# Fewer sums behind the last loads, a new deal of the last stores, and a rearranged order of steps in a fused attention and feed-forward kernel

## The chip, the cores and the metric

The kernel runs on one core of a Trainium2 chip. The metric is the device time of one execution in microseconds (us); the time of a kernel is the median of its runs. Engines are named as in the profile: PE is TensorE's matrix multiplication (PEld its weight loads), DVE is VectorE, ACT is ScalarE, POOL is GpSimd, and SP is SyncE, which here only issues transfers. ACT and POOL issue transfers too.

## The reference

Two layers, one behind the other, on q, k, v of [4, 6080, 256] in fp32, with tau = 1:

```
qn, kn = q / |q| , k / |k|                  # norms over the 6080 tokens, per channel
a      = softmax(kn^T qn / tau, last axis)  # 256 x 256 for each of the 4 batches
x      = v @ a                              # [24320, 256] over all batches
out    = gelu_tanh(x @ w_in) @ w_out        # w_in 256 x 2048, w_out 2048 x 256, out in fp32
```

The kernel computes in bf16 with fp32 sums and uses that x @ w_in = v @ (a @ w_in): for each batch it makes the 256x2048 matrix "aw" = a @ w_in once and multiplies v by it.

## The kernel before

**Blocks.** The 24,320 tokens are cut into 25 blocks: five of 1024 and one of 960 for each batch, the last batch ending in 512 and 448. A block goes through two products. The first, v @ aw followed by gelu, gives g; the second, g @ w_out, gives the output. Both are built mostly by a Strassen-like scheme (fewer products of quarters, more sums): m1 to m7 and the steps with a leading w (wcq, wap, wax, wy5, and wGp, wGs, wGr, wGx, the gelus) belong to the first product, T1 to T4 (sums over tokens), M1 to M7 and cq, y5, ap, ax, c11 to c22 to the second. Some parts of the first product are made plainly: "g.u_x" is a plain product (`plain`), "G.u_x" its gelu. M7 reads the sum T3. In blocks 1 to 22 T3 is made by a transfer on POOL's queue that adds in place (g<-g, `token_sum`, `SUMS_DMA`), everywhere else by DVE. The last block, 24, has a plain second product, `direct` (words "D.p_t").

**Output.** A step c11, c12, c21 or c22 turns a quarter of a block's output by a DVE transpose into an output tile (`turn`, L748; tag "ot", three buffers). When both quarters of a half are in, `store` (L754) issues four transfers of that half, one for each 32 partitions. Before, blocks 0 to 23 store on SP's queue; block 24 has the words sB (half 0) and sA (half 1), each with two stores on SP's queue and two on ACT's, in turn.

**Order.** From the end of the front on, what each engine does and when is not found at run time. A string `ORDER` of some 3,950 words is written out by hand; `run` executes one word after another, and each engine gets its own instructions in that order. A word is "what.arguments@bank:block". Loads of q, k and v for later batches (lq, lk, lv, lt) stand in it as well and wait for the PE instruction that was issued last.

**The front.** The first batch is done by code of its own ahead of ORDER (L791 to L869). q and k come in six chunks of 8, 7, 8, 8, 8, 8 rows (a row is 128 tokens); the last chunk comes in five pieces in the order q 0-3, k 0-4, k 5-7, q 4-5, q 6-7. For each chunk, `gram_row` adds a row's k and q to the gram matrix G on PE; `early_squares` squares q on ACT and k on DVE; `early_fold` (chunks 0 to 3) adds the two halves of the squares on DVE; `ss_rows` sums squares over tokens on PE, 256 columns for a row of k and two single columns for a row of q. Chunk 4's squares are not folded, so it has 8 row sums each for k and q. `warm` issues filler products of 256 columns on PE. Behind the last chunk:

```
scores(0):    lnk, rk from the k sums; lnq, rq from the q sums; S = G * rk; eT = exp(S * rq)
first_aw():   row sums of eT and the first 512 columns of a @ w_in on PE;
              rs = 1 / row sums on DVE; four pieces of aw out of PSUM, (f, ic):
              (0, 0) DVE, (0, 1) ACT, (1, 0) DVE, (1, 1) DVE; each 128 x 256
```

Block 0's first 512 tokens of v are transposed on PE (`pe_vt`), and two copies (`pe_vt_copy`, vT<-vt_ps) bring them to SBUF, both on DVE. ORDER then begins with plain products of block 0 (h<-vT,aw, four groups of 128 columns for each 512 of aw) and with the words aw.p and ac.p, which make and copy the other slices of aw. Its first words are

```
g.3_0@f:0 g.0_0@g:0 g.2_0@a:0 aw.2@b:0 aw.3@c:0 ac.2:0 ac.3:0 g.1_0@d:0 vp.1@z:0 vc.1_1:0 vc.1_0:0
```

Of the kernel before, what the change touches and what calls it, by code (L numbers as in the profile page):

```python
# [16 lines left out]
def kernel(  # L17
# [446 lines left out]
    def pe_vt_copy(n, h, cc):  # L464
        x, y = parts_of(n)[h]
        nc.vector.tensor_copy(vt_tile(n)[:, cc, x:y], VPS[n, h][:, cc, :])
# [277 lines left out]
    def turn(n, ci, tj, src):  # L744
# [6 lines left out]
        if TURNED[n, tj] == 2 and n != LAST:  # L751
            store(n, tj, (nc.sync,) * 4)

    def store(n, tj, engines):  # L754
# [4 lines left out]
        dst = out[r0 : r0 + hc, :].rearrange("(x t) (b c) -> b t x c", t=32, b=4)
        for bi in range(4):  # L760
            engines[bi].dma_start(
                out=dst[bi],
                in_=ot[bi * 32 : bi * 32 + 32, 0 : hc // 32].rearrange("p x h c -> p x (h c)"))
# [197 lines left out]
vp.0@z:1 g.12_1@e:0 g.11_1@a:0 g.10_0@c:0 pA11:0 pS3:0 vc.0_0:1 G.5_1:0 g.6_1@f:0 G.11_1:0 G.4_1:0
G.14_1:0 G.10_0:0 g.8_0@b:0 G.12_1:0 lq.0:1 g.0_1@a:0 g.9_1@d:0 g.15_1@g:0 g.6_0@c:0 g.8_1@e:0
G.0_1:0 G.9_1:0 pF0:0 g.7_1@a:0 lv.1:1 G.6_0:0 G.6_1:0 G.8_1:0 vc.0_1:1 g.13_1@d:0 G.7_1:0 G.13_1:0
pS1:0 SW.1:0 pF1:0 T1.1:0 T1.0:0 pS4:0 M1.1@c:0 g.3_0@f:1 G.15_1:0 g.4_0@e:1 pNA:0 G.4_0:1 lq.1:1
g.15_0@a:0 G.3_0:1 g.12_0@d:1 g.0_0@g:1 M1.0:0 g.11_0@e:0 G.8_0:0 lt.1:1 T2.0:0 g.10_0@f:1 T3.1:0
pA12:0 G.11_0:0 G.12_0:1 G.10_0:1 ksq.0:1 M5.1@b:0 M5.0:0 lv.0:2 y5:0 G.15_0:0 qsq.0:1 row.0_2@z:1
T2.1:0 g.13_0@e:0 f1.0:1 row.0_1:1 row.0_4:1 g.2_0@d:1 g.14_0@f:0 m1.1@b:1 G.0_0:1 G.2_0:1 pS2:0
f2.0:1 vs:1 lq.2:1 g.12_0@a:0 f3.0:1 T3.0:0 g.8_0@g:1 G.14_0:0 G.12_0:0 wcq.1@d:1 row.0_3:1 G.8_0:1
row.0_0:1 g.4_1@f:1 row.0_5:1 m2.1:1 g.7_1@a:1 lk.2:1 G.13_0:0 g.10_1@g:1 G.4_1:1 m1.5@e:1 row.1_3:1
row.1_1:1 row.1_5:1 wGp.1:1 cq@f:0 g.3_1@d:1 row.1_4:1 row.1_0:1 row.1_2:1 G.10_1:1 G.7_1:1 m5.1@g:1  # L970
lq.3:1 G.3_1:1 gc:1 wy5.1:1 wcq.5@a:1 m6.1:1 M6.0:0 m5.5@d:1 M6.1:0 wap.1@g:1 T4.1:0 m2.5:1 wy5.5:1
sp.0@z:1 lv.1:2 wGp.5:1 sa.0:1 ksq.1:1 qsq.1:1 ap@d:0 m6.5:1 M2.0:0 g.15_1@a:1 M2.1:0 lk.3:1 f1.1:1
c11:0 f2.1:1 G.15_1:1 m3.1:1 m7.1:1 g.0_1@a:1 wax.1:1 wGs.1:1 M3.1:0 G.0_1:1 f3.1:1 T4.0:0 g.2_1@g:1
lt.1:2 m1.6@c:1 m5.6@a:1 M7.1:0 sp.1@z:1 m4.1:1 G.2_1:1 lt.0:2 M7.0:0 M3.0:0 wy5.6:1 sa.1:1
g.15_0@g:1 wap.5@a:1 ksq.2:1 m7.5:1 wGr.1:1 qsq.2:1 m3.5:1 lk.4:1 ax:0 f1.2:1 wGx.1:1 wax.5:1
G.15_0:1 M4.1:0 wcq.6@b:1 f2.2:1 g.7_0@g:1 wGs.5:1 c12:0 f3.2:1 m2.6:1 wGx.5:1 m6.6:1 m4.5:1
g.11_1@a:1 G.7_0:1 lq.4:1 wap.6@d:1 M4.0:0 sp.2@z:1 g.11_0@g:1 wGr.5:1 G.11_1:1 wGp.6:1 m7.6:1
g.12_1@e:1 T1.0:1 c21:0 sa.2:1 M5.0@a:1 qsq.3:1 m3.6:1 row.2_0@z:1 wax.6:1 ksq.3:1 G.12_1:1 wGs.6:1
m4.6:1 T1.1:1 g.8_1@b:1 f1.3:1 row.2_3:1 vs:2 wGx.6:1 wGr.6:1 g.0_0@f:2 row.3_2:1 G.11_0:1 G.8_1:1
lv.0:3 g.4_1@e:2 T2.1:1 lk.5:1 m1.3@d:2 G.4_1:2 row.3_1:1 g.4_0@c:2 wcq.3@g:2 M5.1:1 m5.1@b:2  # L980
m5.3@e:2 m2.3:2 G.0_0:2 row.2_5:1 y5:1 T2.0:1 wy5.3:2 G.4_0:2 wy5.1:2 row.2_2:1 m1.1@f:2 m6.3:2
T3.1:1 g.12_0@a:2 row.3_5:1 g.8_1@e:2 row.2_1:1 row.3_0:1 wap.3@c:2 wcq.1@b:2 m6.1:2 row.3_4:1
G.8_1:2 lq.5:1 wap.1@e:2 G.12_0:2 m2.1:2 wGp.3:2 f2.3:1 m7.3:2 row.3_3:1 m3.3:2 wax.3:2 row.2_4:1
M1.0@a:1 m5.2@g:2 m3.1:2 m7.1:2 M1.1:1 gc:1 wGs.3:2 f3.3:1 T4.0:1 lv.1:3 m1.5@c:2 sp.3@z:1 m4.3:2
wGx.3:2 wGp.1:2 wy5.2:2 wGs.1:2 g.12_1@b:2 T3.0:1 wax.1:2 cq@g:1 ksq.4:1 qsq.4:1 m4.1:2 M2.1:1
wGr.3:2 wcq.5@e:2 G.12_1:2 wGr.1:2 m1.2@d:2 m2.5:2 wcq.2@b:2 M2.0:1 m5.5@f:2 lq.6:1 sa.3:1 f1.4:1
m6.2:2 m2.2:2 wGp.5:2 m1.6@e:2 M6.0:1 m6.5:2 wy5.5:2 wcq.6@f:2 lk.6:1 c11:1 wGp.2:2 f2.4:1 wap.2@a:2
T4.1:1 m3.2:2 m7.2:2 m2.6:2 wGx.1:2 wax.2:2 g.0_1@b:2 M6.1:1 wGs.2:2 m4.2:2 wGp.6:2 G.0_1:2
wap.5@a:2 f3.4:1 m6.6:2 ap@f:1 c22:0 wGr.2:2 wGx.2:2 m5.6@b:2 m3.5:2 lt.0:3 sp.4@z:1 ksq.5:1 m7.5:2
m1.7@d:2 M7.1:1 wax.5:2 qsq.5:1 f1.5:1 sa.4:1 f2.5:1 lt.1:3 M3.1:1 M7.0:1 m4.5:2 wGs.5:2 wcq.7@a:2  # L990
wy5.6:2 M3.0:1 m6.7:2 ax:1 m5.7@b:2 f3.5:1 wGr.5:2 wy5.7:2 m2.7:2 sp.5@z:1 M4.0:1 wGx.5:2 wap.6@c:2
sa.5:1 m7.6:2 wap.7@b:2 wax.6:2 qsq.6:1 wGp.7:2 row.4_2@z:1 row.4_3:1 m3.7:2 m7.7:2 c12:1 ksq.6:1
M4.1:1 lk.7:1 wGx.6:2 wGs.7:2 wax.7:2 m3.6:2 row.5_0:1 g.8_0@f:2 m4.6:2 wGs.6:2 row.5_3:1 wGr.6:2
wGx.7:2 row.4_1:1 row.4_0:1 row.5_1:1 row.5_4:1 m4.7:2 row.5_5:1 row.4_4:1 row.4_5:1 m1.1@a:3
m1.2@b:3 G.8_0:2 wGr.7:2 c21:1 wcq.1@c:3 f1.6:1 g.0_0@g:3 g.8_1@e:3 vs:3 f2.6:1 m2.1:3 m5.1@f:3
wcq.2@d:3 lq.7:1 G.8_1:3 T1.0:2 wy5.1:3 row.5_2:1 m2.2:3 m6.1:3 M1.1@e:2 wap.1@f:3 wGp.2:3 wGp.1:3
G.0_0:3 m5.2@d:3 m6.2:3 m3.1:3 m7.1:3 T3.0:2 T1.1:2 g.0_1@c:3 wax.1:3 m1.3@g:3 wy5.2:3 wGs.1:3
G.0_1:3 M5.1@d:2 wap.2@f:3 m5.3@c:3 m3.2:3 m4.1:3 lv.0:4 wGx.1:3 M1.0:2 m7.2:3 f3.6:1 T2.0:2 gc:1
lv.1:4 wy5.3:3 wGr.1:3 wGs.2:3 wcq.3@c:3 wax.2:3 M5.0:2 m2.3:3 sp.6@z:1 cq@a:2 T2.1:2 m5.4@f:3
m4.2:3 y5:2 wGp.3:3 wy5.4:3 m6.3:3 wGr.2:3 wap.3@d:3 qsq.7:1 M2.0:2 M2.1:2 m7.3:3 m1.4@c:3 sa.6:1  # L1000
ksq.7:1 T3.1:2 lv.0:5 c11:2 M6.0:2 m1.5@f:3 m3.3:3 wcq.4@b:3 T4.0:2 m2.4:3 wGx.2:3 wax.3:3 wcq.5@e:3
# [333 lines left out]
```

## Time and the profile before

| what | us |
|---|---|
| median of 3 runs (lowest to highest) | 683.48 (683.37 to 683.81) |
| the profiled execution | 684.09 |
| its span, from the first to the last instruction | 682.3 |
| first plain product (h) starts | 38.23 |
| last product of PE ends | 675.7 |
| last stores: issued on ACT / SP from | 675.36 / 677.62 |

The profile is one execution, of 684.09 us, with 1.79 us around its span. A row of the timeline gives start, busy time, engine, line, operation, the tile written and the tiles read, sizes, count, and in brackets the idle time ahead of the group and what ended it. The windows give busy time and, in brackets, instructions of each engine in a stretch, then the granted PE clock (1.00 is full), the DMA share and GB/s. The tail of the span is in us: PE is done at 675.7, and what is left is turning and storing block 24.

### The profile page before, as it was taken

Reading aid. Unit: us, or ns where it says so; the run is one execution under the profiler, and the core shown is the slowest. Engines: PE = TensorE matmul, PEld = TensorE weight load, DVE = VectorE, ACT = ScalarE, POOL = GpSimd, SP = SyncE. Lnnn points to the kernel's source line nnn. Section 1 sums busy time; section 2 is a strip of 40 time slices with the busy share of each in tenths; the row PEclk is TensorE's granted clock in tenths of the full one; section 3 lists DMA queues with packets and bytes.
Section 4 is the critical chain, followed back from the end, with each engine's and each line's share of the span. In section 5 each row is a group of like instructions: output and inputs, shape, how many; then the busy total and the mean of one; then the engine's idle time right before and its main releaser. Section 6 shows DMA issues by size and latency. Waiting matters only on the chain.

```text
span 682.3 us, 10610 instructions
## 1 busy us (share of the span) xinstructions
PE 663.0 (97%) x3579; PEld 336.3 (49%) x3579; DVE 612.2 (90%) x941; ACT 621.5 (91%) x1193; POOL 112.4 (16%) x177
## 2 busy tenths in 40 slices
...
GB/s 240 208 256 126 151 180 167 178 165 136 175 151 175 171 164 155 175 80 166 129 135 169 175 167 197 134 134 150 69 148 115 101 151 147 101 107 152 81 84 96
DMA packets 168807, 101.70 MB, mean 149 GB/s; under 512 B 150240, under 2 KB 153952, under 8 KB 168032
## 3 DMA queue, kind: packets, MB, share of 16 engines
...
q14 instruction: 27, 0.22, 0.1%
...
## 4 chain that ended last, share of the span: by engine, by line
PE 93%; DMA 3%; DVE 2%; ACT 0%; issue 0%; SPq 0%; POOL 0%; DVEq 0%; POOLq 0%
PE rb L481 18%; PE p L481 17%; PE q L481 15%; PE r L481 11%; PE h L481 10%; PE m L481 10%; PE G L205 6%; PE awp L375 2%; DMA qk_f<-in_q_dram 1%; DMA g<-g 1%; PE o L481 1%; PE warm L269 1%; PE ss L263 1%; DVE t L700 0%; DMA vT<-vb 0%; DVE q L622 0%
## 5 line engine op out<-in xcount | busy, mean ns | idle before, releaser
L481 PEld LDWEIGHTS <-wcomb 128*128 128x128 bf16 x1408 | 136.6, 98 | 144.9 <-issue 3.4
L631 ACT ACTIVATE g<-q 128x512 bf16<-128x512 f32 (+1 forms) x286 | 169.4, 623 | 5.7 <-PE q L481 5.1
L481 PEld LDWEIGHTS <-aw 128*128 128x128 bf16 x807 | 77.9, 98 | 77.1 <-DVE aw L415 1.3
L622 DVE TENSOR_TENSOR q<-rb,yw 128x512 f32<-128x512 f32 (+2 forms) x150 | 102.4, 687 | 13.3 <-PE rb L481 4.4
L700 DVE TENSOR_TENSOR t<-g,t 128x2048 bf16<-128x2048 bf16 (+2 forms) x96 | 112.7, 1180 | 0.1
L625 DVE TENSOR_TENSOR xw<-rb,yw 128x512 f32<-128x512 f32 (+2 forms) x150 | 101.5, 678 | 10.1 <-PE rb L481 7.5
L481 PE MATMUL rb<-tv,sw 128*128 128x512 bf16 (+3 forms) x314 | 109.2, 367 | 0.0
L539 ACT ACTIVATE g<-h 128x512 bf16<-128x512 f32 (+1 forms) x164 | 97.1, 650 | 5.3 <-PE h L481 5.1
L619 ACT ACTIVATE yw<-m 128x512 f32<-128x512 f32 (+2 forms) x150 | 93.0, 626 | 3.9 <-PE m L481 2.9
L481 PE MATMUL p<-t,wcomb 128*128 128x512 bf16 (+2 forms) x384 | 95.5, 373 | 0.0
L631 ACT ACTIVATE g<-xw 128x512 bf16<-128x512 f32 (+1 forms) x143 | 92.6, 650 | 2.7 <-DVE xw L625 2.3
L613 ACT ACTIVATE q<-rb 128x512 f32<-128x512 f32 (+2 forms) x150 | 90.6, 614 | 4.7 <-PE rb L481 3.0
L481 PE MATMUL r<-g,wcomb 128*128 128x512 bf16 (+2 forms) x384 | 94.7, 373 | 0.0
L481 PE MATMUL h<-vT,aw 128*128 128x512 bf16 (+2 forms) x336 | 93.5, 377 | 0.8 <-DVE aw L415 0.8
L481 PEld LDWEIGHTS <-sw 128*128 128x128 bf16 x628 | 61.2, 98 | 61.8 <-issue 1.2
L631 ACT ACTIVATE g<-rb 128x512 bf16<-128x512 f32 (+1 forms) x143 | 87.7, 619 | 2.5 <-PE rb L481 2.1
L694 POOL DMA_DIRECT2D g<-g x44 | 39.7, 917 | 196.3 <-ACT g L631 92.0
L700 DVE TENSOR_TENSOR t<-g 128x2048 bf16<-128x2048 bf16 (+2 forms) x48 | 56.4, 1184 | 1.6 <-ACT g L539 1.3
L481 PE MATMUL q<-vT,sw 128*128 128x512 bf16 (+3 forms) x157 | 56.2, 367 | 0.0
L481 PE MATMUL q<-vT,aw 128*128 128x512 bf16 (+3 forms) x157 | 55.8, 367 | 0.0
L481 PE MATMUL rb<-vT,aw 128*128 128x512 bf16 (+3 forms) x157 | 55.7, 367 | 0.0
L481 PE MATMUL m<-tv,sw 128*128 128x512 bf16 (+3 forms) x157 | 55.7, 367 | 0.0
...
## 6 DMA issues: line engine op xcount, KB each, us to landing
...
wst<-in_moe_w_out_dram POOLq DMA_DIRECT2D x2, 1024.0 KB, 10.4
```

What stands on the lines that cost most here:

```text
L205: nc.tensor.matmul(G[b][:, jc, :], lhsT=qt[:np_, r, jc * 128 : jc * 128 + 128], rhs=kt[:np_, r, :], start=first and jc == 0, stop=jc == 1, ...
L263: nc.tensor.matmul(SS[1], lhsT=ones_bf, rhs=sq[:, 256:512], start=c == 0 and r == 0, stop=end)
L375: nc.tensor.matmul(ps, lhsT=ET[b][:, jc, ic * 128 : ic * 128 + 128], rhs=win_bf[:, jc, fs * 512 : fs * 512 + 512], start=jc == 0, stop=jc ...
L481: GATE[0] = nc.tensor.matmul(*a, skip_group_check=True, **kw)
L539: nc.scalar.activation(g_half(n, u // 8)[:, x, u % 8], hp[:, :hc], AF.Gelu_apprx_tanh)
L613: nc.scalar.activation(Q[n, i, 0][:, :w], RB[n, i][:, :w], AF.Copy)
L619: nc.scalar.activation(YW[n, i][:, :w], M5.pop((n, i))[:, :w], AF.Copy)
L622: nc.vector.tensor_add(Q[n, i, 1][:, :w], RB[n, i][:, :w], YW[n, i][:, :w])
L625: nc.vector.tensor_add(XW[n, i][:, :w], RB[n, i][:, :w], YW.pop((n, i))[:, :w])
L631: nc.scalar.activation(g[:, t, k0], x[:, :w], AF.Gelu_apprx_tanh)
L694: nc.gpsimd.dma_start(out=o, in_=quarter(n, 1, 1, h), accum_op=ALU.add)
L700: (nc.vector.tensor_add if add else nc.vector.tensor_sub)(o, a, b)
```

## The change

1. `early_fold_k`: the two halves of chunk 4's squares of k are added on DVE, and chunk 4 has 4 row sums of k where it had 8.
2. Chunk 5: the k sums 0-4 and 5-7 stand behind gram rows 0-3, the q sums 0-5 come in one go behind rows 4 and 5.
3. `warm(8)` becomes `warm(6)`.
4. The second of the two copies of block 0's transposed v goes from DVE to ACT.
5. `token_sum` can make T2 by an accumulating transfer as well, for the blocks in `SUMS2_DMA`, which is empty.
6. `direct` gives each quarter of block 24's half 1 a bank of its own (words "D.p_1_m").
7. Stores: of block 23's half 1, stores 0 and 2 stay with SP at the turn, and 1 and 3 go to ACT at the word c11:24. In block 24, sB is all on SP's queue, and sA has three stores on ACT's and one on SP's.
8. ORDER is rearranged: its first 500 words, several stretches in the middle, and its end. It holds the same products; between the stretches it is the same word for word. Block 0 now begins with the plain products of column groups 0 and 1 of aw (g.0_0, g.1_0).

```diff
+    def early_fold_k(c):
+        k = [x[:, :, 256:512] for x in SQ[c]]
+        nc.vector.tensor_add(k[0], k[0], k[1])
...
+    def pe_vt_copy(n, h, cc, eng="dve"):
...
+        if eng == "act":
+            nc.scalar.activation(o, i, AF.Copy)
+        else:
+            nc.vector.tensor_copy(o, i)
...
-            store(n, tj, (nc.sync,) * 4)
+            store(n, tj, (nc.sync, None) * 2 if (n, tj) == (LAST - 1, 1) else (nc.sync,) * 4)
...
-            store(n, 1 if what == "sA" else 0, (nc.sync, nc.scalar, nc.sync, nc.scalar))
+            store(n, 1 if what == "sA" else 0, (nc.sync,) * 4 if what == "sB" else (nc.scalar,) * 3 + (nc.sync,))
...
+            if n == LAST and what == "c11":
+                store(LAST - 1, 1, (None, nc.scalar) * 2)
             if n == LAST:
-                src = ACC[n, tj][:, ci * hc : ci * hc + hc]
+                src = ACC[n, tj, ci] if tj else ACC[n, tj][:, ci * hc : ci * hc + hc]
...
             if c < nch - 2:
                 early_fold(c)
+            else:
+                early_fold_k(c)
...
-        ss_rows(c - 1, 1)
+        ss_rows(c - 1, 1, range(0, 4))
         ss_rows(c - 1, 0)
         early_squares(c, 0, 0, 4, "act")
         early_squares(c, 1, 0, 5, "dve")
         for i in range(4):
             gram_row(0, c, i)
-        ss_rows(c, 0, range(0, 4))
+        early_squares(c, 1, 5, 8, "dve")
         ss_rows(c, 1, range(0, 5))
-        early_squares(c, 1, 5, 8, "dve")
+        ss_rows(c, 1, range(5, 8))
         early_squares(c, 0, 4, 6, "dve")
-        ss_rows(c, 1, range(5, 8))
         for i in (4, 5):
             gram_row(0, c, i)
-        ss_rows(c, 0, range(4, 6))
+        ss_rows(c, 0, range(0, 6))
...
-        warm(8)
+        warm(6)
         pe_vt(0, 0, "e")
         scores(0)
         pe_vt_copy(0, 0, 0)
-        pe_vt_copy(0, 0, 1)
+        pe_vt_copy(0, 0, 1, "act")
         first_aw()
...
+SUMS2_DMA = {}
...
 ORDER = """
-g.3_0@f:0 g.0_0@g:0 g.2_0@a:0 aw.2@b:0 aw.3@c:0 ac.2:0 ac.3:0 g.1_0@d:0 vp.1@z:0 vc.1_1:0 vc.1_0:0
+g.0_0@f:0 g.1_0@g:0 g.3_0@a:0 aw.2@b:0 G.1_0:0 g.2_0@e:0 aw.3@c:0 ac.2:0 ac.3:0 vp.1@z:0 g.4_0@d:0
...
-D.7_1:24 c11:24 c21:24 c12:24 sB:24 c22:24 sA:24
...
+D.5_1_1:24 D.2_0:24 c21:24 D.3_1_0:24 D.4_1_0:24 c11:24 D.1_1_1:24 D.5_1_0:24 D.3_1_1:24 D.6_1_0:24
+D.2_1_0:24 D.6_1_1:24 D.2_1_1:24 c12:24 sB:24 c22:24 sA:24
```

More of the change, by code (lines that the diff above doesn't have):

```diff
@@ L687, in token_sum @@
         hc = hc_of(n)
+        by_dma = n in (SUMS_DMA if i == 3 else SUMS2_DMA if i == 2 else ())
         if i == 3:
             o = quarter(n, 0, 1, h)
-        else:
-            o = tp.tile([128, 4, 512], BF16, tag="tx" if i in (1, 4) else "ty", name=f"t{i}{h}_{n}")[:, :, :hc]
+        elif i == 2 and by_dma:
+            o = TS[n, 1, h]
+        else:
+            x = i == 1 or i == 4 and n not in SUMS2_DMA
+            o = tp.tile([128, 4, 512], BF16, tag="tx" if x else "ty", name=f"t{i}{h}_{n}")[:, :, :hc]
         TS[n, i, h] = o
-        if i == 3 and n in SUMS_DMA:
+        if by_dma:
             nc.gpsimd.dma_start(out=o, in_=quarter(n, 1, 1, h), accum_op=ALU.add)
@@ L726, in next_sum, with direct @@
         fill(ACC[n, acc], tag, hc)
-    def direct(n, p, t, tag):
+    def direct(n, p, t, *mt):
         hc = hc_of(n)
-        for m in range(2):
-            first = (n, t) not in ACC
+        *ms, tag = mt
+        key = (n, t, *ms)
+        for m in ms or range(2):
+            first = key not in ACC
             if first:
-                ACC[n, t] = bank(tag, [128, 512], f"o{n}_{t}")
+                ACC[key] = bank(tag, [128, 512], f"o{n}_{t}_{m}")
                 BITS[tag] = 2 * hc
+            x0 = 0 if ms else m * hc
             for fc in (2 * p, 2 * p + 1):
                 w = ((A11, A12), (A21, A22))[m][fc // 8]
-                mm(ACC[n, t][:, m * hc : m * hc + hc], lhsT=wcomb[:, w, fc % 8, :],
+                mm(ACC[key][:, x0 : x0 + hc], lhsT=wcomb[:, w, fc % 8, :],
                    rhs=GT[n, fc // 8][:, t, fc % 8],
@@ L757, in store @@
         r0 = b * N + t0 + tj * hc
-        ot = OT.pop((n, tj))
+        ot = OT[n, tj]
         dst = out[r0 : r0 + hc, :].rearrange("(x t) (b c) -> b t x c", t=32, b=4)
         for bi in range(4):
-            engines[bi].dma_start(
-                out=dst[bi],
-                in_=ot[bi * 32 : bi * 32 + 32, 0 : hc // 32].rearrange("p x h c -> p x (h c)"))
+            if engines[bi] is not None:
+                engines[bi].dma_start(
+                    out=dst[bi],
+                    in_=ot[bi * 32 : bi * 32 + 32, 0 : hc // 32].rearrange("p x h c -> p x (h c)"))
     def mm2_step(n, what, tag):
@@ L961 @@
[L961 to L1001, printed above, removed]
@@ new lines @@
+M3.1:0 m4.5:1 qsq.2:1 g.12_1@e:1 wGp.6:1 ax:0 lq.4:1 m6.6:1 sa.1:1 ksq.2:1 wap.6@f:1 M4.0:0
+g.8_1@b:1 wGx.5:1 m7.6:1 wGr.5:1 f1.2:1 lq.5:1 wax.6:1 M3.0:0 g.11_1@g:1 G.8_1:1 f2.2:1 m3.6:1
+m4.6:1 G.12_1:1 wGx.6:1 G.11_1:1 c12:0 g.7_0@b:1 f3.2:1 M4.1:0 sp.2@z:1 lk.4:1 wGr.6:1 g.8_1@e:2
+g.4_0@d:2 vs:2 sa.2:1 m1.3@g:2 wGs.6:1 G.7_0:1 m5.3@c:2 g.12_0@f:2 row.2_2@z:1 T1.0:1 G.8_1:2 T3.0:1
+T1.1:1 wcq.3@b:2 wy5.3:2 G.4_0:2 row.2_5:1 m1.1@e:2 row.3_1:1 row.3_4:1 m6.3:2 row.3_0:1 c21:0
+m5.1@c:2 row.2_4:1 G.12_0:2 wcq.1@d:2 wap.3@f:2 lk.5:1 row.2_1:1 m2.1:2 qsq.3:1 m2.3:2 m7.3:2
@@ new lines @@
+ksq.4:1 m2.5:2 M2.0:1 wGs.2:2 wax.2:2 m4.2:2 f1.4:1 sa.3:1 m1.6@d:2 lk.6:1 M2.1:1 wGp.5:2 wGx.2:2
+wGr.2:2 ap@e:1 f2.4:1 wap.5@a:2 M7.0:1 f3.4:1 sp.4@z:1 wcq.6@b:2 qsq.5:1 M3.0:1 m7.5:2 c11:1 c22:0
+m2.6:2 ksq.5:1 lt.0:3 m3.5:2 m5.6@c:2 m6.6:2 wy5.6:2 wGs.5:2 M7.1:1 wax.5:2 m1.7@c:2 m4.5:2 f1.5:1
+wap.6@a:2 wGp.6:2 f2.5:1 wGr.5:2 wcq.7@b:2 wGx.5:2 M3.1:1 sa.4:1 f3.5:1 m7.6:2 m5.7@g:2 lt.1:3
+m3.6:2 m6.7:2 ax:1 wax.6:2 wy5.7:2 sp.5@z:1 m2.7:2 sa.5:1 M4.1:1 m4.6:2 c12:1 wap.7@g:2 M4.0:1
+T1.0:2 lk.7:1 c21:1 wGp.7:2 wGr.6:2 wGx.6:2 m3.7:2 g.8_0@b:2 row.5_0@z:1 m7.7:2 wGs.6:2 wax.7:2
@@ new lines @@
+wap.1@a:6 wcq.2@e:6 lq.3:2 wGr.3:6 m2.2:6 wGp.2:6 m5.2@c:6 m6.2:6 m7.1:6 wy5.2:6 m3.1:6 M6.1:5
+wGx.3:6 wGs.1:6 g.12_0@e:6 m5.5@c:6 M6.0:5 lk.3:2 G.12_0:6 g.12_1@a:6 c11:5 c22:4 f1.1:2 wax.1:6
+m4.1:6 wap.2@b:6 wy5.5:6 wGx.1:6 G.12_1:6 wGr.1:6 m1.5@e:6 m7.2:6 ap@c:5 M3.1:5 m3.2:6 wcq.5@a:6
+wax.2:6 wGs.2:6 m4.2:6 m6.5:6 m2.5:6 wGr.2:6 wGp.5:6 m5.6@g:6 T4.1:5 M3.0:5 wGx.2:6 wap.5@b:6 f2.1:2
+c12:5 m7.5:6 wax.5:6 m1.7@f:6 m3.5:6 row.1_3:2 m1.6@a:6 M7.1:5 wy5.6:6 m4.5:6 wcq.6@c:6 lk.4:2
+wGs.5:6 row.0_0:2 m6.6:6 wGr.5:6 m5.7@g:6 wcq.7@b:6 T4.0:5 M7.0:5 m2.6:6 wGx.5:6 f3.1:2 wap.6@e:6
@@ new lines @@
+wap.6@e:11 M6.0:10 m4.5:11 row.0_3@z:3 m6.7:11 m2.7:11 wy5.7:11 lv.1:14 ap@d:10 m3.6:11 m7.6:11
+row.0_4:3 wGr.5:11 M7.1:10 wGx.5:11 wGp.7:11 wap.7@g:11 wax.6:11 T4.1:10 m3.7:11 m4.6:11 m7.7:11
+M3.0:10 wGx.6:11 wax.7:11 c22:9 wGr.6:11 g.4_1@f:12 wGs.7:11 wGs.6:11 SW.0:2 M7.0:10 G.4_1:12 ax:10
+g.0_1@b:12 m1.3@g:12 G.0_1:12 m4.7:11 g.8_0@e:12 m1.1@f:12 wGr.7:11 wcq.1@b:12 wcq.3@a:12 M3.1:10
+vs:12 lt.1:13 G.8_0:12 M4.0:10 m2.1:12 m5.3@e:12 c12:10 m6.3:12 wGx.7:11 wy5.3:12 wGp.1:12 T1.1:11
+wap.3@d:12 lt.0:13 m2.3:12 M4.1:10 m5.1@e:12 g.0_0@b:12 m3.3:12 wGp.3:12 T1.0:11 G.0_0:12 m7.3:12
@@ new lines @@
+wcq.3@a:13 m1.5@c:13 sp.2@z:3 y5:12 c11:12 wcq.5@d:13 sa.2:3 m2.3:13 m6.3:13 m4.2:13 ksq.3:3 M6.0:12
+m6.5:13 m2.5:13 row.2_1@z:3 m1.6@f:13 wGp.3:13 wGr.2:13 wap.3@a:13 m3.3:13 row.2_0:3 m7.3:13
+wap.5@e:13 m3.5:13 wGx.2:13 M6.1:12 wGp.5:13 T4.1:12 lq.4:3 wcq.6@d:13 wGs.3:13 m6.6:13 m7.5:13
+row.3_4:3 wax.3:13 row.3_2:3 wGs.5:13 ap@a:12 T4.0:12 m4.3:13 m5.6@e:13 qsq.3:3 m2.6:13 M3.0:12
+wy5.6:13 lk.5:3 wGx.3:13 M3.1:12 wGp.6:13 wGr.3:13 wap.6@e:13 wax.5:13 c12:12 m7.6:13 row.3_0:3
+m5.7@d:13 m4.5:13 m1.7@b:13 g.4_1@a:13 M7.1:12 wGx.5:13 wGr.5:13 wcq.7@c:13 c22:11 wy5.7:13 wax.6:13
@@ new lines @@
+wap.3@e:14 ap@d:13 f3.4:3 m7.3:14 c11:13 lt.0:15 lt.1:15 m3.3:14 m1.6@b:14 wGs.3:14 wcq.6@g:14
+M3.1:13 sp.4@z:3 wax.3:14 qsq.5:3 M7.1:13 m6.6:14 m5.7@e:14 ksq.5:3 wy5.7:14 M7.0:13 m4.3:14
+wap.6@c:14 lv.1:16 f1.5:3 m2.6:14 m7.6:14 m1.7@e:14 ax:13 m3.6:14 wGr.3:14 wcq.7@a:14 wGx.3:14
+wGs.6:14 f2.5:3 sa.4:3 M3.0:13 M4.1:13 f3.5:3 c12:13 wax.6:14 sp.5@z:3 g.12_0@c:14 m2.7:14 m6.7:14
+wGp.6:14 M4.0:13 lq.7:3 qsq.6:3 sa.5:3 ksq.6:3 row.4_5@z:3 g.4_0@d:14 row.5_0:3 wap.7@g:14 m7.7:14
+m4.6:14 row.5_2:3 m3.7:14 row.5_1:3 wGx.6:14 f1.6:3 row.4_0:3 wGp.7:14 G.12_0:14 row.5_5:3
@@ new lines @@
+sa.7:3 T4.1:14 wy5.6:15 lv.0:17 m1.6@c:15 m7.4:15 pow:3 m5.7@b:15 m3.4:15 wax.4:15 wcq.6@g:15
+lv.0:18 wGs.4:15 M7.0:14 m4.4:15 m6.6:15 c12:14 ax:14 wap.6@a:15 m1.7@d:15 wy5.7:15 wGr.4:15
+g.0_0@b:15 m2.6:15 wcq.7@e:15 G.0_0:15 row.6_5@z:3 row.7_1:3 c22:14 m6.7:15 row.6_3:3 m7.6:15
+row.7_2:3 wGx.4:15 wGp.6:15 m3.6:15 M4.0:14 wap.7@b:15 wax.6:15 wGs.6:15 wGx.6:15 m7.7:15 m3.7:15
+m4.6:15 m1.1@g:16 lv.1:18 kf:3 wax.7:15 kr:3 M4.1:14 wGs.7:15 m4.7:15 wcq.1@a:16 wGr.6:15 T1.0:15
+row.7_3:3 g.0_1@b:16 m2.7:15 row.7_0:3 m2.1:16 wGx.7:15 T3.0:15 G.0_1:16 wGp.7:15 vs:16 c21:14
@@ new lines @@
+M5.0:17 wGp.4:18 wGx.2:18 m5.5@z:18 T2.1:17 m1.5@c:18 m7.4:18 wcq.5@e:18 M6.0:17 m4.3:18 m3.4:18
+m2.5:18 m6.5:18 y5:17 wax.4:18 wy5.5:18 wGr.3:18 M6.1:17 m4.4:18 wap.5@b:18 m3.5:18 m5.6@z:18
+ap@f:17 wGp.5:18 wGs.4:18 wGs.5:18 wy5.6:18 m1.7@e:18 T4.0:17 wGr.4:18 m7.5:18 m1.6@d:18 M3.0:17
+m5.7@z:18 M3.1:17 wcq.6@b:18 wcq.7@a:18 m6.6:18 wGx.4:18 wax.5:18 T4.1:17 c22:16 m2.7:18 m4.5:18
+m2.6:18 m6.7:18 M7.1:17 wy5.7:18 wGp.6:18 wGr.5:18 wGx.5:18 c12:17 wap.6@b:18 M7.0:17 wap.7@f:18
+ax:17 m7.6:18 g.0_0@c:19 m7.7:18 m3.7:18 M4.0:17 wGp.7:18 wGx.3:18 wGs.7:18 G.0_0:19 m3.6:18
```

596 lines of the change are left out of this document (295 added, 301 removed).

## The prediction

> **What bounds the kernel.** The page first: TensorE is busy 97% of the span and carries the chain that ended last.
>
> ```profile
> span 682.3 us, 10610 instructions
> PE 663.0 (97%) x3579; PEld 336.3 (49%) x3579; DVE 612.2 (90%) x941; ACT 621.5 (91%) x1193; POOL 112.4 (16%) x177
> PE 93%; DMA 3%; DVE 2%; ACT 0%; issue 0%; SPq 0%; POOL 0%; DVEq 0%; POOLq 0%
> ```
>
> The windows by stage say where PE is not full.
>
> ```profile
> core 0: us, PE busy (x) PEld busy (x) DVE busy (x) ACT busy (x) POOL busy (x), PEclk, DMA share, GB/s
> 20.20:38.20 18.00, 17.27 (x204) 14.86 (x202) 8.89 (x19) 8.32 (x13) 8.12 (x11) 1.00 1.19 206
> 60.00:120.00 60.00, 60.00 (x337) 30.91 (x335) 58.76 (x92) 57.39 (x105) 12.28 (x21) 1.00 0.96 161
> 120.00:140.00 20.00, 19.32 (x99) 8.93 (x98) 19.06 (x31) 18.18 (x37) 3.82 (x7) 1.00 0.85 155
> 140.00:500.00 360.00, 359.96 (x1853) 175.09 (x1852) 344.86 (x530) 346.95 (x675) 62.13 (x94) 1.00 0.88 153
> 660.00:675.70 15.70, 15.70 (x149) 14.18 (x147) 10.49 (x21) 9.23 (x21) 0.00 (x0) 1.00 0.60 101
> 675.70:682.30 6.60, 0.02 (x1) 0.00 (x0) 0.71 (x2) 0.00 (x0) 0.00 (x0) 0.75 0.42 71
> ```
>
> From 39 to 675.7 PE has one wait that the waits list shows:
>
> ```profile
> 131.28 1.02 PE L481 MATMUL p<-g,wcomb 128*128 128x512 bf16 x4 [0.68 <-DMA g<-g]
> ```
>
> The new order holds the same products, so three things can move the end: the start of the first h, new or vanished waits between, and the 6.6 us behind PE's last product.
>
> **The front.** Timeline of 34 to 40 us:
>
> ```profile
> 34.83 1.03 PE L269 MATMUL warm<-zeros_bf,ones_bf 128*128 128x256 bf16 x8
> 35.01 0.26 ACT L281 ACTIVATE lnq<-ss,eps 128x2 f32<-128x2 f32 x1
> 35.63 0.91 ACT L289 ACTIVATE eT<-S,rq 128x256 bf16<-128x256 f32 x2
> 36.35 0.76 DVE L466 COPY vT<-vt_ps 128x512 bf16<-128x512 bf16 x2 [0.59 <-PE vt_ps L461]
> 37.02 0.16 DVE L405 RECIPROCAL rs<-sums 128x2 f32<-128x2 f32 x1
> 37.28 0.47 ACT L413 ACTIVATE aw<-aw_ps,rs 128x256 bf16<-128x256 f32 x1 [0.74 <-DVE rs L405]
> 37.30 1.27 DVE L415 TENSOR_SCALAR aw<-aw_ps,rs 128x256 bf16<-128x256 f32 x3
> 38.23 1.64 PE L481 MATMUL h<-vT,aw 128*128 128x512 bf16 x6 [0.76 <-DVE aw L415]
> ```
>
> The chain is: last q sum, lnq, rq, eT, row sums, rs, aw pieces, first h. DVE's two vT copies hold rs: the row sums end at 36.80, rs starts at 37.02.
>
> - *Fold of chunk 4's k.* One DVE addition of 128x1024: 0.65 to 0.68 us by the 128x1024 additions of L700 late in the run. DVE idles 1.63 us before its next square at 31.70, so it is hidden. Chunk 4's k sums then start at about 30.75, not 30.54, but there are 4 fewer of 0.109 us; PE waits for chunk 5's q (landed 31.63) either way and starts on it about 0.15 earlier.
> - *Order in chunk 5.* k sums 0-7 stand ahead of rows 4-7 and the q sums come in one go. The last k sum ends at about 33.60 (33.92 before). But the last q piece lands at 33.91 and its square ends at 34.36 as before, so by adding 0.060 us a matmul the last q sum ends 0.11 earlier: eT ends at 36.43, the row sums at 36.69.
> - *Two warm fillers fewer* take 0.22 us off PE: the v transposes end near 36.0 (before 36.3; v landed at 35.19), and DVE's one vT copy runs 36.03 to 36.45.
> - *The other vT copy on ACT*, which is free between eT (36.43) and its aw piece: 36.45 to about 36.95, taking the 0.47 us of ACT's 128x256 piece as the nearest row and a little more for 512 bf16 columns. DVE then is free at the row sums: rs at 36.73 to 36.80, 0.22 to 0.29 earlier.
> - *First h.* Before, its first word was a block in the second half of the slice, whose piece is DVE's second (second matmul: third piece), so h starts at 38.23 and its third matmul at 38.85. Now the first words, g.0_0 and g.1_0, read the first half: DVE's first piece (done 37.5 to 37.56) and ACT's (37.5). First h at 37.55 to 37.62, third matmul at about 38.0: 0.80 to 0.87 gained. The three w_in loads, v's second half and w_out land 0.4 us or more before their users in the new places (37.85 against 38.85 is the first), so none takes over. PE's idle stretch ahead of the first h is no longer than before (0.76), and the granted clock is 1.00 in every window from 20.2 to 675.7, so I cost the clock at nothing.
> - *Given back:* g.4_0 needs the slice that DVE copies after aw.3 (0.75 us a copy, its end near 41.1): a stall of 0.35, where before one of 0.15 stood ahead of g.7_0: 0.2 lost.
>
> Front: 0.83 - 0.2 = 0.63 gained; bounds 0.2 (ACT's copy late by one piece of 0.47) and 0.9.
>
> **The middle.** ORDER is changed in its first 500 words, in some stretches of the middle and at its end; between these it is word for word the same. PE's columns there are equal but for two pads more (32 and 192 columns, 0.09 us). The shortest distances in PE time between a product and the sums that it feeds are the same in both orders. Two things get tighter. The accumulating transfers g<-g (T3, on POOL's queue; median 6.4 us to landing, 4.6 to 9.3 in all) stand 9.2 us ahead of their M7 in block 5, 9.5 in 15, 9.7 in 1, and 10.5 to 11.2 in 13 and 14, where before it was 12 to 18. And the first rows of batch 1's gram stand 6.5 us behind the step that releases their load (before 9.5 or more); those loads took 4.55 to 6.6. The wait at 131.28 (a transfer of 8.76 us) has the same words around it and stays. Bounds: 0.8 gained, if that wait goes, and 2 lost, if two transfers of 9 us or longer meet the short distances; I take the pads alone, 0.09 lost, since the median transfer is 2.8 us inside the shortest distance. SUMS2_DMA is empty, so token_sum does what it did.
>
> **The tail.** Rows of the last products and the three store groups on the queues of ACT and SP:
>
> ```profile
> 671.73 4.00 PE L481 MATMUL o<-g,wcomb 128*128 128x224 bf16 x40
> 675.36 2.07 ACTq L761 DMA_DIRECT2D out_dram<-ot  x4
> 675.76 0.71 DVE L748 STREAM_TRANSPOSE ot<-o 128x224 f32<-128x224 f32 x2 [0.44 <-PE o L481]
> 677.62 2.02 SPq L761 DMA_DIRECT2D out_dram<-ot  x4
> ```
>
> SP is idle from 674.28 to 677.56: its first store of block 24 shares its landing semaphore with ACT's store issued at 675.75, which lands at 677.54. Four more stores, 0.36 to 0.5 apart, end the issue at 679.21; the last lands at 680.98, and the span ends 1.33 later.
>
> In the new deal ACT takes two stores of block 23 as soon as its last gelu is done (672.8 and 673.2; landing +1.75: 674.5 and 674.95). SP's fourth store of block 23's first half waits for the first of these, from about 670 to 674.55. Queued behind it on SP: two stores of block 23, four of sB, one of sA. Eight stores, 0.48 apart, from 674.55: the last is issued at 677.9 to 678.5 and lands 1.75 later, 679.7 to 680.3. The output buffers (three) also chain DVE: c12 of block 24 must wait until block 23's first half has landed (676.45), so c22 ends at 677.25, before 676.47; ACT's three stores of sA follow at 677.3 to 678.15 and land at 679.9. Both queues end near 679.95: 1.0 gained. On PE, M4 of block 23 needs a sum that DVE ends at about 666.6 in the new place, 0.4 ahead: nothing, 0.2 lost at most. Bounds: 1.6 gained (0.36 apart throughout) and 0.47 lost (below).
>
> **Sum.** -0.63 - 1.0 + 0.09 = -1.54. The profiled execution took 684.09 us (span 682.3 and 1.79 around it), 0.61 above the median of 683.48; the difference is put on the median: 681.9. A measurement of this kernel tells about 0.2%, 1.37 us: faster is below 682.1, slower above 684.85.
>
> **Rivals.**
> - *The two queues share one rate* (no change): stores of one queue land about 0.5 us apart, and the DMA share of 660 to 675.7 is 0.60. If SP and ACT together place one store per 0.5 us, the eleven stores from 674.55 end at 679.65, the last lands at 681.45, 0.47 later than now; total -0.07: 683.4. For it: spacing grows from 0.36 to 0.5 within a group. Against: DMA share is only 0.42 in the last 6.6 us, and before, ACT's stores at 676.51 and 677.11 still landed within 1.8. Chance 0.21. The Trainium skill, "DMA: Bandwidth & Descriptors", section "Issuing engines are not separate DMA queues", speaks for this rival: DMAs of all issuing engines interleave on the same 16 DMA engines, and a second issuer saves only the time to issue. By that rule the time would be this rival's; the landing times of before do not show the queues slowing each other.
> - *Late accumulating transfers* (slower): M7 waits in blocks 1, 5 and 13 to 15, where T3 stands 9.7, 9.2 and 10.9, 10.5, 11.2 and 9.5 us ahead. At 10.7 us a transfer PE waits 1.0 + 1.5 + 0.2 + 1.2 = 3.9 us, which gives 685.8; from about 10.4 us on (2.9 in all) the kernel ends slower than before by over 1.37. For: the transfer at 122.48 took 8.76 us and held PE, another took 9.3, and with DVE and ACT at 58.8 and 57.4 of 60 us little is left to catch up. Against: the median of 6.4. Chance 0.13.
> - *The front gains nothing*, since the copy on ACT or the fold turns out on the path: 683.48 - 1.0 + 0.09 = 682.6. Chance 0.08.
>
> **Numbers.** Forecast case 0.58, own range 680.7 to 682.6. The low end of the range has front and tail at their best and the wait at 131 gone (683.48 - 0.9 - 1.6 + 0.09 - 0.7 = 680.4); the high end has the shared rate, the front at its least and one late transfer of 0.5 us (683.48 + 0.47 - 0.2 + 0.09 + 0.5 = 684.3). Faster 0.53 (0.50 of the forecast case, 0.03 from rivals with the wait at 131 gone), same 0.34, slower 0.13.
>
> **Right or wrong.** Right: first h near 37.6, its third matmul near 38.0; no DVE idle ahead of rs; no PE wait over 0.3 between 42 and 675 but that near 131; SP held until about 674.5, then eight stores; c12 near 676.5; last landing 4.3 us behind PE's end, not 5.3. Wrong: a PE wait on g<-g in blocks 1, 5 or 13-15; a store on one queue that takes over 2.5 us while the other issues; a granted clock under 1.00 behind 30 us.

## The result and the profile after

Over 22 runs each, the changed kernel took 684.89 us in the median (683.49 to 689.50), the kernel before 683.80 (683.30 to 684.43): 1.0023 times the time before, with a 95% interval from 1.0012 to 1.0033. It became slower by 1.1 us where 1.5 less was forecast. Its profiled execution took 685.01 us with a span of 683.2, against 684.09 and 682.3 before. So the two profiles differ by 0.9 us, close to the difference of the medians, and can be compared step by step.

The page of the changed kernel:

```profile
span 683.2 us, 10566 instructions
PE 659.6 (97%) x3513; PEld 335.7 (49%) x3575; DVE 612.7 (90%) x941; ACT 623.3 (91%) x1194; POOL 113.1 (17%) x177
PE 85%; DMA 8%; ACT 3%; DVE 2%; issue 1%; SPq 0%; DVEq 0%; POOL 0%; ACTq 0%; POOLq 0%
```

PE shows 62 matmuls fewer than weight loads (PEld): records that are missing from this trace, one every 10 us or so, not idle time. PE's busy time can therefore not be compared with before; starts can. The third line has the news: the chain that ended last now runs through DMA for 8% of the span, 3% before.

The waits between 38 and 676 us, the lines of PE and of DVE's transposes:

```profile
DVE ot L765 <- DMA out_dram<-ot: 1.7, 1, 1.7
PE rb L489 <- DVE q L630: 1.3, 2, 1.1
DVE ot L765 <- PE rb L489: 0.9, 1, 0.9
PE h L489 <- DVE ot L765: 0.7, 1, 0.7
```

In the profile before, PE's one wait of that stretch was on an accumulating transfer (g<-g); that one is gone, and there are two new ones that hang on DVE's output transposes. Rows of SP's queue, DVE and PE from the timelines of the two places:

```profile
365.38 10.24 SPq L780 DMA_DIRECT2D out_dram<-ot  x6
376.45 0.68 DVE L765 STREAM_TRANSPOSE ot<-q 128x480 f32<-128x480 f32 x1 [1.67 <-DMA out_dram<-ot]
377.27 0.70 DVE L630 TENSOR_TENSOR q<-rb,yw 128x512 f32<-128x512 f32 x1
378.02 0.38 PE L489 MATMUL rb<-tv,sw 128*128 128x512 bf16 x1 [1.07 <-DVE q L630]
380.29 0.38 PE L489 MATMUL rb<-tv,sw 128*128 128x512 bf16 x1 [0.21 <-DVE q L630]
...
403.16 0.72 DVE L765 STREAM_TRANSPOSE ot<-q 128x512 f32<-128x512 f32 x1 [0.88 <-PE rb L489]
403.93 0.59 PE L489 MATMUL h<-vT,aw 128*128 128x512 bf16 x2 [0.70 <-DVE ot L765]
```

At 376 us, DVE's c12 of block 11 wants an output buffer. There are three; the one whose turn it is holds block 10's half 0, and its four stores, issued from 364.41 to 366.64, land only at 372.7 to 376.4. These stores are set off by c21 of block 10, which the change had moved 42 words later in ORDER, while c12 of block 11 stayed in its place. DVE stands for 1.67 us, behind it in DVE's order stands wap of block 12, and for that PE waits 1.24 and then 0.38 us (start to start, less the matmul itself). At 403 us the same happens to c12 of block 12: the waits list names PE as releaser, but that product was long done, while the last store of the buffer lands at 402.94. PE loses 0.87 us.

To see where the time went, I count from the end how much product work (columns) is left on PE, and compare the times at which the same amount is left:

| stretch | changed less before, us, at its end | what happens in it |
|---|---|---|
| to 42.6 | -0.51 | first h earlier |
| to 122.7 | -0.05 | short waits of PE for ACT at 63 to 70 and 99.6 (0.4 in all) |
| to 138.6 | -0.90 | the wait near 131 is gone |
| to 365 | -0.95 | nothing |
| to 380 | +0.66 | the buffer wait of block 11 |
| to 410 | +1.48 | the buffer wait of block 12 |
| PE's end | +1.30 | nothing much |
| span | +0.92 | the tail is 0.38 shorter |

The tail of the changed kernel (timeline):

```profile
672.45 4.57 PE L489 MATMUL o<-g,wcomb 128*128 128x224 bf16 x46
672.94 0.35 ACTq L780 DMA_DIRECT2D out_dram<-ot  x1
677.47 0.71 DVE L765 STREAM_TRANSPOSE ot<-o 128x224 f32<-128x224 f32 x2 [1.42 <-DMA out_dram<-ot]
678.21 1.34 ACTq L780 DMA_DIRECT2D out_dram<-ot  x3
```

PE ends at 677.0, the last store lands at 681.88, 4.9 behind; before it was 5.3. So the tail did gain, and the loss lies at the two places in the middle.

### The profile page after: what moved, and what is told of

Its sections match the earlier page's. It is cut to its first block, busy times and chain, and to the rows that moved or that the text cites. A ratio compares the mean times of both kernels' runs of the same rounds, so it can differ in the third digit from the quotient of the medians.

```text
span 683.2 us, 10566 instructions
## 1 busy us (share of the span) xinstructions
PE 659.6 (97%) x3513; PEld 335.7 (49%) x3575; DVE 612.7 (90%) x941; ACT 623.3 (91%) x1194; POOL 113.1 (17%) x177
## 4 chain that ended last, share of the span: by engine, by line
PE 85%; DMA 8%; ACT 3%; DVE 2%; issue 1%; SPq 0%; DVEq 0%; POOL 0%; ACTq 0%; POOLq 0%
PE rb L489 17%; PE p L489 16%; PE q L489 14%; PE r L489 11%; PE m L489 10%; PE h L489 10%; DMA out_dram<-ot 4%; PE G L205 4%; DMA qk_g1b<-in_k_dram 3%; PE awp L379 2%; DMA qk_g1a<-in_q_dram 1%; ACT g L639 1%; DVE ot L765 1%; SPq L780 0%; ACT q L621 0%
## 5 line engine op out<-in xcount | busy, mean ns | idle before, releaser
L489 PE MATMUL h<-vT,aw 128*128 128x512 bf16 (+2 forms) x320 | 89.4, 377 | 1.6 <-DVE ot L765 0.7
## 6 DMA issues: line engine op xcount, KB each, us to landing
wst<-in_moe_w_out_dram POOLq DMA_DIRECT2D x2, 1024.0 KB, 10.5
```

The lines of the kernel that those rows point to most:

```text
L489: GATE[0] = nc.tensor.matmul(*a, skip_group_check=True, **kw)
```

## Experiments

Two theories are tried here. **R (ring)** comes from the waits above: the rearranged words of blocks 1 to 18 put DVE's turns closer to the stores that must free their buffer; where those land late, DVE stands, and PE behind it. **L (landing semaphores)** comes from e3 below: the stores of SP and ACT share eight semaphores that tell of their landing; a store on SP's queue that has one of ACT's ahead of it on its semaphore holds the whole queue until that one has landed. Rivals were the front (A), DVE's own load or the accumulating transfers (D), and chance (C). Medians are given against the kernel before on the same chip; kernels that mix both orders keep the words of each and only rename banks.

**e1, the middle of before.** Words 600 to 3100 of ORDER as before, all else changed.

> The changed kernel with words 600 to 3100 of ORDER taken from the kernel before; front, first 600 words and tail stay changed. Theory R (ring: DVE's turns wait for an output buffer whose stores land late, since the new order of blocks 1 to 18 puts them closer, and PE waits behind): the front's gain of 0.5 and the tail's of 0.4 remain and nothing is lost, so 0.9 below the kernel before, about 682.9, and all runs within 1 us of each other. Rival A (front: loads and first-batch steps that now start earlier push later ones late, whatever the order of the middle): 684.5 or more, runs spread over several us.

682.91 against 684.00 (0.9989; 0.9978 to 0.9999). In its profile PE's end is 0.93 ahead of before and no wait hangs on a turn. R holds; A falls as the cause of the loss in the median. One of 11 runs took 686.78, so not all were within 1 us.

**e4, blocks 11 to 13 of before.** Words 1902 to 2400 as before, all else changed.

> The changed kernel with words 1902 to 2400 of ORDER (blocks 11 to 13, around 335 to 420 us) from the kernel before. Theory R: the waits at 378 and 404 us of the profile go, 682.4 to 683.2, and the spread of the runs falls to what other stretches leave. If the same waits turn up at other places in other runs, 684 and a spread of 2 us or more stays.

682.33 against 684.00 (0.9982; 0.9971 to 0.9992), a little better than expected. PE's end is 2.36 earlier than in the changed kernel: the whole loss of the middle lies in this stretch.

**e2 and e3, four output buffers.** `name="yout", bufs=3` becomes 4, in the changed kernel and in that before; to make room, the tile DN takes the tag "S".

> The changed kernel with four output buffers (tag ot) instead of three; to make room, the denominators of the softmax share the buffer of the scores. Theory R: the two waits of DVE for stores (1.24 + 0.38 and 0.87 us on PE in the profile) go, so 2.1 to 2.5 below the changed kernel, 682.3 to 682.8, with a spread under 1.2 us. Rival D (DVE or the accumulating transfers are late by themselves in the new order): 684.4 to 685, spread as with three buffers.

> The kernel before with four output buffers, as a control of the same edit. Theory R: the kernel before has no such wait in its profile, so 683.8 give or take 0.4. Rival D: the same. If it falls by 1 us or more, the fourth buffer gives something else than the waits named.

e2: 683.49 against 684.00 (1.0003; 0.9991 to 1.0015), above the 682.3 to 682.8 expected. Both waits are gone from the profile, as R says, and PE's end is 3.05 ahead of the changed kernel, but the span is only 1.6 shorter. e3: 686.56 (1.0045; 1.0028 to 1.0063), where nothing was expected to move; PE's end is 0.26 later. Both lost their time behind PE's end. SP's waits at the end of e3 (waits, 660 to 686 us):

```profile
SPq L761 <- DVE ot L748: 11.7, 3, 9.6
SPq L761 <- DMA out_dram<-ot: 7.7, 1, 7.7
```

With another buffer the stores' semaphores are dealt otherwise. SP issues nothing between its stores of 669.14 and 677.35, until a store that ACT issues at 675.62 has landed at 677.33; ten stores stand in its queue meanwhile. Before, the same line reads 3.3 us, in the changed kernel 4.5. This is where L comes from; neither R nor D had foreseen it. By its time e2 is no test of R; by its waits it is.

**e5, the front alone**, with words 0 to 600.

> The kernel before with the changed front and words 0 to 600 of the changed ORDER; blocks after that, and the stores, as before. Theory R: 0.5 gained at the first h, 0.4 given back in waits of PE for ACT between 60 and 100 us, 0.85 gained since the wait near 131 us is gone whenever the changed first 600 words are in (it was gone in the three profiles that had them); 0.95 below the kernel before in all, 682.9 to 683.2. Rival C (the wait near 131 comes and goes by chance): 683.7, and the wait is in the profile.

683.39 against 683.92 (0.9995; 0.9987 to 1.0003): between the two. In the profile all of the 0.93 is there at PE's end, with the wait near 131 gone; by the medians 0.5 is. That wait was in every profile with the old first 600 words (before, e3, e6, e11, e14) and in none with the new: C falls. The second accumulating transfer of block 2 took 7.84 us here and 8.76 before, and lands at 129.77, 0.35 ahead of its M7.

**e14, the middle alone.** Words 600 to 3100 as changed, all else before.

> The kernel before with words 600 to 3100 of the changed ORDER alone; front, first 600 words, end and stores as before. Theory R: 1.6 lost near 378 and 0.9 near 404 and nothing gained: 2.0 to 2.6 above the kernel before, 685.8 to 686.4. Rival A (the loss comes only together with the changed front, which runs 1 us ahead of the loads): 683.8 to 684.5.

685.37 against 683.61 (1.0028; 1.0017 to 1.0039), 1.8 above and somewhat less than expected. Its waits from 38 to 676 us, PE's and those of the turns on stores:

```profile
DVE ot L748 <- DMA out_dram<-ot: 1.7, 1, 1.7
PE rb L481 <- DVE q L622: 1.3, 2, 1.1
PE p L481 <- DMA g<-g: 1.2, 1, 1.2
```

The same waits without the changed front: R again. With the old front, the wait near 131 is there as well (p <- g<-g), longer than before.

**e7, one step earlier.** In ORDER, c21:10 moves 23 places forward (the expectation counts 24), to the ninth place behind M4.1:10.

> The changed kernel with one word of ORDER moved: c21 of block 10 stands 24 words earlier, so that its half's stores are issued 4.4 us earlier. Theory R: DVE's c12 of block 11 finds its buffer free and PE's waits at 378 to 380 us (1.6) go, while that at 404 (0.87) stays: 683.1 to 683.6. Rival D (DVE is behind in blocks 11 to 13 by its own work): unchanged, 684.5 to 685.2.

683.26 against 683.92 (0.9998; 0.9983 to 1.0012), inside the expected 683.1 to 683.6. The waits at 378 and 380 us are gone from the profile, that at 402 is still there with 0.76. Moving one word, whose step PE needs for nothing but the buffer, is worth 1.6 us.

**e9 and e10, a second step.** c21:11 moves 19 words forward too; e10 has all stores on SP as well.

> The kernel of e7 with a second word moved: c21 of block 11 stands 19 words earlier, so that its half's stores are issued 2.1 us earlier and ahead of the two accumulating transfers of block 12. Theory R: the wait at 404 us (0.75 in e7) goes too; 0.5 to 0.9 below e7 (683.26), 682.4 to 682.8. Rival K (the stores land late because k, v and the accumulating transfers crowd them, wherever they are issued): the wait stays, 683.0 to 683.5.

> The kernel of e9 with all stores on SP's queue as in e8. Theories R and L together: 0.2 to 0.7 below e9 and equal to e8 (682.16) within 0.4. If R fails at 404 us: 682.8 or more.

A miss: 683.91 and 683.35 against 683.75 (1.0005; 0.9994 to 1.0015, and 1.0005; 0.9989 to 1.0021). c21:11 now stands ahead of a sum (wap) that PE needs, and on DVE it must itself wait 0.38 us for its product: a new wait of PE of 0.66 at 385 us in both. The wait at 402 stays in e9 (0.75) and is gone in e10, in the same order of words: the last stores of the buffer land at 401.82 in the one and at 400.00 in the other. So the second step did not help, and what a store takes to land there differs between profiles.

**e13, no accumulating transfers in block 12.** e7 with 12 taken out of SUMS_DMA.

> The kernel of e7 with the sum T3 of block 12 made by DVE (two additions of some 1.2 us) and not by two accumulating transfers of 512 KB. Theory K (stores that are issued among these transfers, the loads of v and k land behind them): the stores of block 11's first half land in 3 to 6 us and not in 9 to 15, and the buffer wait at 402 us is not in the profile; DVE's added 2.4 us may cost PE up to 1 us there, so 682.4 to 683.6 in time. Rival (the stores are late for another reason, such as the loads alone): they still take 9 us or more and the wait of 0.75 stays.

685.03 against 683.61 (1.0021; 1.0010 to 1.0032): DVE's added work costs PE 2.0 us, more than expected, but the buffer wait is gone. DMA issues between 384 and 392 us (KB each, median us to landing), e7 first:

```profile
g<-g POOLq DMA_DIRECT2D x2, 512.0 KB, 8.5
out_dram<-ot SPq DMA_DIRECT2D x4, 120.0 KB, 9.2
k<-in_k_dram POOLq DMA_DIRECT2D x1, 384.0 KB, 10.8
vb<-in_v_dram POOLq DMA_DIRECT2D x1, 256.0 KB, 11.7
```

```profile
out_dram<-ot SPq DMA_DIRECT2D x4, 120.0 KB, 3.1
k<-in_k_dram POOLq DMA_DIRECT2D x1, 384.0 KB, 5.0
vb<-in_v_dram POOLq DMA_DIRECT2D x1, 256.0 KB, 3.8
```

Without the two 512 KB transfers on POOL's queue, the stores on SP's queue land in a third of the time; the loads of k and v are still there, so they alone are not the reason. For the stores of block 10, late in the wait at 376 us, this was not tried. The Trainium skill, "DMA: Bandwidth & Descriptors", section "Issuing engines are not separate DMA queues", says that DMAs of all issuing engines run on the same 16 DMA engines and interleave; these two views agree.

**e6, the tail alone.** Words from 3100 on, `direct` and the deal of the stores as changed.

> The kernel before with the changed stores, direct products and words of ORDER from 3100 on. Theory R: as in the profile of the changed kernel, 0.4 gained behind PE's end: 683.3 to 683.6; ACT's first store lands 2.6 to 2.9 us after issue and SP's eight stores start right behind it. The prediction's sum: 1.0 gained, 683.0. Rival S (two queues share one rate): 683.8 or more.

683.90 against 683.92 (1.0000; 0.9991 to 1.0009): nothing gained, which is the time of rival S and not that of R or of the prediction's sum. ACT's first store lands 3.06 us after its issue, and SP waits for it from 669.8 to 674.7.

**e8 and e11, all stores on SP.** e4 and e6 with `(nc.sync,) * 4` for block 23 and for sA and sB.

> The kernel of e4 (blocks 11 to 13 in the order of before) with all stores on SP's queue, so that no store of SP waits for one of ACT. Theory L (what delays the end is that SP's queue stands behind a store of ACT with which it shares a landing semaphore): SP issues 23's stores by 672.5 and block 24's as soon as they are turned, the last at about 677.0; 0.7 below e4, 681.4 to 681.9. Rival Q (one queue is too slow for the last eight stores, and two are needed): 0.5 or more above e4, 682.8 or more.

> The kernel of e6 (front and middle of before, changed end) with all stores on SP's queue. Theory L: PE's end stays where it was, and the end follows PE's last product by 5.9 us as in e8 and not by 7.0 as in e6; 682.6 to 683.3 against 683.9 for e6. Rival Q (e8's gain came from its middle): 683.9.

e8: 682.16 against 683.92 (0.9974; 0.9964 to 0.9984), all 7 runs within 0.4, the lowest median of the study. That is above the range of L, and 0.2 below e4, or 0.1 when each is set against the kernel before on its own chip. (The profiles of the two differ by 0.7, but e4's was of a run 0.5 above its median.) e11: 683.26 against 683.75 (0.9991; 0.9983 to 1.0000), 0.6 below e6, within the range of L; the intervals of e6 and e11 overlap. SP's waits at the end of e8 (660 to 682 us):

```profile
SPq L780 <- DVE ot L765: 12.8, 4, 10.3
SPq L1356 <- DMA out_dram<-ot: 1.3, 1, 1.3
```

No store of SP waits for another to land any more; what is left is the end of the kernel (L1356). So one queue is not slower than two, and Q falls. But the gain is not made where L puts it. Times behind PE's end, in us:

| kernel | queues | c22 turned | last store of SP issued | its landing takes | it has landed |
|---|---|---|---|---|---|
| before | two, one after the other | 0.75 | 3.49 | 1.77 | 5.26 |
| changed | two at once | 1.16 | 2.33 | 2.52 | 4.86 |
| e4 | two at once | 1.36 | 2.52 | 2.37 | 4.89 |
| e6 | two at once | 1.55 | 2.72 | 2.65 | 5.37 |
| e8 | SP alone | 0.46 | 2.55 | 1.80 | 4.35 |
| e11 | SP alone | 0.46 | 3.01 | 1.80 | 4.80 |

Without the hold, c12 and c22 are turned 0.9 to 1.1 us sooner; but SP then issues the last four stores in a row, and its last one stands no earlier (e8) or 0.3 later (e11). All of the gain is in the landing. The last stores of e6 and of e11, as the DMA view lists them (count, KB each, us to landing):

```profile
out_dram<-ot ACTq DMA_DIRECT2D x1, 56.0 KB, 2.7
out_dram<-ot SPq DMA_DIRECT2D x1, 56.0 KB, 2.7
```

```profile
out_dram<-ot SPq DMA_DIRECT2D x1, 56.0 KB, 1.8
```

Where ACT and SP store at the same time, the last stores take 2.3 to 2.7 us and not 1.8: that is rival S in part. An instruction load of 8 KB falls into these landings too, but where one met stores of SP alone they took 1.7 to 2.1 (before, e3, e8, e11). Taking ACT's stores away ends the hold and the sharing together, and no run parts the two. What a hold costs by itself is seen in e3, where ten stores were held: the last store lands 7.95 us behind PE's end, against 5.26 before. The size is uncertain as well: e1, with two queues, ends 5.9 us after the start of PE's last matmul, as e8 does, against 6.4 in e11, 6.5 in e4 and 7.0 in e6.

**e12, the copy back on DVE**, in e5 (one run: 683.41).

> The kernel of e5 (changed front alone) with the second copy of the transposed v back on DVE. The prediction's step: rs starts behind two DVE copies at 36.8 or later, so the first h is 0.1 or more later than in e5 on the same scale (from eT's end: 1.15 there). Rival: with two fillers fewer the copies end before the row sums do, and the first h comes at the same time within 0.05.

Timelines of the front, e5 first, then e12:

```profile
35.42 0.91 ACT L293 ACTIVATE eT<-S,rq 128x256 bf16<-128x256 f32 x2
36.62 0.17 DVE L409 RECIPROCAL rs<-sums 128x2 f32<-128x2 f32 x1 [0.28 <-PE sums L406]
37.45 1.47 PE L489 MATMUL h<-vT,aw 128*128 128x512 bf16 x6 [0.19 <-DVE aw L419]
```

```profile
35.29 0.91 ACT L293 ACTIVATE eT<-S,rq 128x256 bf16<-128x256 f32 x2
35.79 0.76 DVE L474 COPY vT<-vt_ps 128x512 bf16<-128x512 bf16 x2 [0.38 <-PE vt_ps L465]
36.49 0.17 DVE L409 RECIPROCAL rs<-sums 128x2 f32<-128x2 f32 x1
37.31 1.47 PE L489 MATMUL h<-vT,aw 128*128 128x512 bf16 x6 [0.18 <-DVE aw L419]
```

From eT's start to the first h it is 2.03 in e5 and 2.02 here (2.60 before). Before, rs started 0.22 us behind the end of the row sums; it starts 0.04 behind it in both of these. With two fillers fewer the copies are early enough not to hold rs, and moving one to ACT gains nothing.

## Why the prediction was wrong, step by step

- **First h, third matmul, stall at g.4_0:** right. In the changed kernel the weights are loaded at 37.59 and matmuls follow at 37.82, 38.03 and every 0.216 on; six are needed, five are recorded, so the first is missing and began at 37.60 (37.55 to 37.62 forecast), the third at 38.03. The stall is 0.35 at 41.20, as said. Of the reasons, the copy on ACT was none (e12), and DVE is idle for 0.28 us ahead of rs, where no idle time was forecast: it waits for the row sums. (The landing at 31.6 us, read as chunk 5's q, is its k 0-4; the q had landed at 30.07. Nothing hangs on it.)
- **Front, 0.63 gained:** 0.51 by 42.6 us. What failed is what came behind it: 0.4 went to PE waiting for ACT in the reordered first batch, where I had followed DVE's steps alone.
- **Middle, "the pads alone, 0.09 lost":** this is the step that failed. It weighed two resources, the accumulating transfers and the loads of k and q, and checked distances between products and sums. The ring of three output buffers was not among them, so waits for it were put at nothing without a reason. Nor was it a matter of some stretches: between words 612 and 3099, 2003 of the 2488 stand at another place than before. Counted in PE time, from the step that issues a half's stores to the first turn that reuses its buffer, c12 of block 11 had 17.2 us before and 10.4 after; stores of 128 KB landed in up to 10.5 us in the profile there. c12 of block 12 has more than before (14.5, before 10.9), but its stores are now issued within 2 us of two accumulating transfers, and three of the four take 9 to 14 us. The middle cost 2.4 us at these two places, and the wait near 131 us, which I took to stay, went with the new first words: +1.6 net. That the buffer waits make the loss is shown (e1, e4, e7, e14); why the wait near 131 went is not: in e5 the transfer took 7.84 us instead of 8.76.
- **The rival of late transfers** had the right sign, a time near the measured one (685.8) and the wrong victim: no M7 waits in the changed kernel. The transfers made stores late instead, for block 12 at least (e13). That its time came near is luck.
- **Tail, 1.0 gained:** 0.40 in the changed kernel, nothing alone (e6). The chain ran as written (SP held, eight stores, c12 held by its buffer). ACT's first store takes 2.67 us, not 1.75, and the eight SP stores stand 0.53 apart, not 0.48, but ACT's first store was also issued 4.1 us ahead of PE's end and not 2.9. So the last issue, 2.33 us behind PE's end, came in the forecast 2.2 to 2.8. The mis-sized term is the last landing: 2.52 us and not 1.75 while ACT stores too. That is a part of the rival of one shared rate, and the sign of being wrong that names it, a store of over 2.5 us while the other queue issues, came: stores of 2.81 and 2.52 us on SP, 2.89 and 2.62 on ACT. The argument against it, that ACT's stores landed within 1.8 before, was no test: SP issued nothing while ACT issued those.
- **The range** was given as 680.7 to 682.6, but its own sums for the two ends are 680.4 and 684.3; 684.89 lies above both. (Ten gaps of 0.5 us from 674.55 end at 679.55, not at 679.65.)
